# Gate rows and second modulation columns of an adaptive-layernorm block: from TensorE matmuls to VectorE partial products and GpSimd sums over partitions

## Chip, cores, metric

One core of a Trainium2 chip. The metric is the device time of one execution in microseconds (us). Every run here is listed in the state "fast" and with a granted TensorE clock of 1.0 (0.999 in one execution of the kernel before). The profile is one execution taken by the hardware profiler; its span is 1.7 to 1.9 us shorter than the device time.

Ratios are the mean time of one kernel's fast runs over the mean of the other's fast runs of the same rounds, so they are not quite the ratios of the medians quoted beside them. Kernels of one batch ran on the same chip and share the runs of the kernel before.

## The reference

```python
mod = (_silu(c) @ w_mod).reshape(c.shape[0], 6, 1, -1)     # c: 1 x 512, w_mod: 512 x 3072
sa, ca, ga, sb, cb, gb = (mod[:, i].copy() for i in range(6))
h = _layernorm(x, axis=-1) * (1 + ca) + sa                 # x: 1 x 2048 x 512
x = x + ga * _A_ref(h, A_k_cache, A_v_cache, A_wq, A_wo)   # attention, 32 heads, window of 512 keys
h = _layernorm(x, axis=-1) * (1 + cb) + sb
x = x + gb * _B_ref(h, B_w1, B_w2)                         # relu MLP, 512 -> 1792 -> 512
```

(The line with `mod[:, i]` is shortened from six assignments.) The first pair, sa and ca, is needed at once. The gate ga is needed when the first block of 512 rows leaves the output projection, sb and cb before the second layernorm, and gb in the MLP. The change is about these four.

## The kernel before

The attention is a loop of 128 steps, one for each head and block of 512 rows. In a step TensorE makes the scores of head s in two halves, the queries of head s+2, the value product of head s-1, and up to four matmuls from a background queue (`bgq`), mostly the output projection. ScalarE makes the exponentials. VectorE reads the value product out of PSUM, and there is only one place for it (`o_ps`, banks 5 and 6).

```python
def mod_cols_mm(which, bk):          # 32 matmuls of one column: weights stationary, silu(c) moving
    ...
                    fs.append(lambda sl=sl, c2=c2, cc=cc, col=idx * DC + c2, last=last: mm(
                        bank[bk][:, col:col + 1], wm[sl][:, cc, c2 * P:(c2 + 1) * P], sc_bf[:, cc:cc + 1],
                        cc == 0, cc == DC - 1, [R_sc, wm_res(sl, cc)], [bk], last))

def mod_row(j):                      # 4 matmuls of 512 columns: silu(c), repeated 128 times, stationary
    sl, dst, r = (2, gaf, R_ga) if j == 0 else (5, gbf, R_gb)
    for cc in range(DC):
        bgq.append(lambda cc=cc: mm(bank[WBK], sc_rep[:, cc, :], wm[sl][:, cc, :], cc == 0, cc == DC - 1, [R_screp, R_wm[sl]], [WBK], cc == DC - 1))
    evac(lambda: kb.op(DVE, lambda e: e.tensor_copy(dst[:, :], bank[WBK]), reads=[R_b[WBK]], writes=[r]))

def pv_mms(u):                       # value product and its read-out
    ...
    kb.op(DVE, lambda e: e.reciprocal(rinv[:, u, :], o_ps[:, :, P]), ...)
    kb.op(DVE, lambda e: e.tensor_tensor(o_sb[u % NOS][:, :, :], o_ps[:, :, 0:P], ..., op=ALU.mult), ...)
    dma(oT[u % NOT][:, :, :], o_sb[u % NOS]..., transpose=True)

def ln_dmaT():                       # the normalised rows, transposed by DMA
    dma(xnT[...], xn[...], "xnT", reads=R_xn, writes=[R_xnT], transpose=True)

for s in range(NU):
    run_tasks(s, 100)                # VectorE work and loads that are due at step s
    if s == 4:
        mods2()                      # mod_row(0), mod_cols_mm(1, WBK), mod_row(1) into bgq
    ...
    s_mms(s, 0)
    if s + QA < NU:
        q_mms(s + QA)
    s_mms(s, 1)
    if s >= 1:
        pv_mms(s - 1)
    pop_bg(4)
```

`kb.op` records an instruction on an engine's stream with the semaphore waits that its reads and writes need. VectorE takes its stream in order, as the traces show: in the changed kernel a value product ends at 207.85 us, VectorE stands until 209.10 in front of a normalisation, and the reciprocal that reads this product, next in the stream, starts only at 209.75.

## Time and profile before

| | |
|---|---|
| time, median of 4 | 564.17 us (564.06 to 564.25) |
| span of the profile | 562.5 us |
| TensorE / ScalarE / VectorE / GpSimd busy | 553.7 / 350.4 / 242.2 / 38.7 us |

The prediction below shows the page's busy row, the chain that ended last, the groups by shape and the timeline. Two things help in reading them. A reciprocal (`rinv<-psO`) with "idle ... <-PE psO" in brackets started when the value product ended, so the distance between two such rows is the length of a step. A reciprocal without a bracket found VectorE late: the engine came from other work, and TensorE may be waiting for it.

### The profile page before, as it was taken

To read this page: it belongs to the slowest core of one execution; us is meant where nothing else is said; L and a number is where in the kernel's file an instruction comes from. 1 tells how busy PE (TensorE), PEld (TensorE's weight loads), DVE (VectorE), ACT (ScalarE), POOL (GpSimd) and SP (SyncE) were. 2 spreads that over 40 slices of the span, in tenths; PEclk is the share of its full clock that TensorE was granted. 3 is DMA by queue.
4 is the path that set the end of the run, shared out by engine and by line. 5 is a ranking of instruction groups with operands and counts; after the bars stand their busy time and mean duration, and the time that the engine had idled before them with its cause. 6 is when DMAs were issued, how large, how long until landed. Compare 5 with 4: busy or idle time off the path is not lost.

```text
span 562.5 us, 9700 instructions
## 1 busy us (share of the span) xinstructions
PE 553.7 (98%) x4097; PEld 316.9 (56%) x4172; DVE 242.2 (43%) x533; ACT 350.4 (62%) x453; POOL 38.7 (7%) x42
## 2 busy tenths in 40 slices
PE   8999999999999999999999999999999999999998
PEld 3565555555555555555555555555555654444444
DVE  4444465533334655333346553333354448321134
ACT  5986666666666666666666666666666644432500
POOL 1000000003300000033000000330000000000000
PEclk9999999999999999999999999999999999999999
DMA  9778776421331247332523522121123220210001
GB/s 268 204 165 167 143 160 132 113 38 38 39 76 37 39 93 133 57 94 46 144 56 57 102 50 39 39 40 40 39 39 72 44 31 0 41 36 24 22 28 48
DMA packets 113310, 42.70 MB, mean 76 GB/s; under 512 B 93928, under 2 KB 112104, under 8 KB 113256
## 3 DMA queue, kind: packets, MB, share of 16 engines
q1 hardware_dynamic: 112024, 40.82, 35.2%
q10 hardware_dynamic: 1232, 1.15, 0.6%
q8 instruction: 35, 0.57, 0.5%
q14 instruction: 19, 0.16, 0.1%
HBM read 18.35 MB, written 2.10 MB: 36 GB/s over the span
## 4 chain that ended last, share of the span: by engine, by line
PE 97%; issue 1%; DMA 1%; DVE 1%
PE psS L1363 28%; PE psO L1363 26%; PE psQ L1363 23%; PE psW L1363 20%; DMA x<-in_A_x_dram 1%; DVE st L1373 0%; PE psS L1366 0%; DVE mv L1374 0%; DVE rstd L1574 0%; DVE PT L1673 0%; DVE PT L1675 0%; DVE tmp L1427 0%; DVE sc_bf L1428 0%; DVE tmp L1426 0%
## 5 line engine op out<-in xcount | busy, mean ns | idle before, releaser
L1482 ACT ACTIVATE PT<-psS 128x1024 bf16<-128x1024 f32 x256 | 262.6, 1028 | 129.5 <-PE psS L1363 129.4
L1363 PE MATMUL psS<-qT,kT 128*128 128x512 bf16 x509 | 151.1, 379 | 0.2
L1363 PEld LDWEIGHTS psO<-v,PT 128*128 128x128 bf16 x2048 | 126.6, 98 | 30.2
L1363 PE MATMUL psO<-v,PT 128*128 128x129 bf16 x2048 | 137.0, 220 | 0.0
L1363 PE MATMUL psQ<-hT,wq 128*128 128x512 bf16 x507 | 130.3, 379 | 0.1
L1492 DVE RECIPROCAL rinv<-psO 128x4 f32<-128x4 f32 x128 | 23.4, 183 | 233.1 <-PE psO L1363 233.1
L1363 PE MATMUL psW<-wo,oT 128*128 128x512 bf16 x451 | 117.9, 379 | 3.2
L1493 DVE TENSOR_TENSOR o<-psO,rinv 128x512 bf16<-128x512 f32 x128 | 88.5, 692 | 4.4
L1363 PEld LDWEIGHTS psQ<-hT,wq 128*128 128x128 bf16 x508 | 49.6, 98 | 60.7 <-issue 0.5
L1363 PEld LDWEIGHTS psS<-qT,kT 128*128 128x128 bf16 x512 | 49.6, 98 | 59.3 <-ACT PT L1482 0.7
L1474 ACT ACTIVATE qT<-psQ 128x512 bf16<-128x512 f32 x127 | 75.2, 592 | 0.5 <-PE psQ L1363 0.5
L1662 ACT ACTIVATE wq<-psS 128x512 bf16<-128x512 f32 x56 | 33.4, 597 | 49.6 <-PE psS L1363 49.6
L1363 PEld LDWEIGHTS psW<-wo,oT 128*128 128x128 bf16 x512 | 45.0, 98 | 32.9 <-DVE acc L1515 1.2
L1515 DVE TENSOR_TENSOR acc<-psW,acc 128x512 f32<-128x512 f32 x48 | 33.2, 691 | 6.7 <-PE psW L1363 6.7
L1363 PE MATMUL psO<-wmw,wq 128*128 128x512 bf16 (+1 forms) x164 | 32.7, 352 | 0.3
L1518 POOL TENSOR_TENSOR acc<-acc,gaf 128x512 f32<-128x512 f32 x12 | 15.3, 1272 | 168.7 <-DVE acc L1515 168.7
L1379 POOL TENSOR_TENSOR rstd<-rstd,cst 128x4 f32<-128x4 f32 x7 | 7.1, 1012 | 265.3 <-DVE rstd L1378 265.3
L1363 PE MATMUL psS<-h2T,wmw 128*128 128x512 bf16 x110 | 25.2, 379 | 0.1
L1673 DVE TENSOR_TENSOR PT<-psO,gbf 128x512 f32<-128x512 f32 (+1 forms) x12 | 7.5, 624 | 40.4 <-PE psO L1363 40.4
L1363 PEld LDWEIGHTS psO<-wmw,wq 128*128 128x128 bf16 x168 | 15.4, 98 | 16.5
L1363 PE MATMUL psS<-hT,wmw 128*128 128x512 bf16 x110 | 24.4, 379 | 0.1
L1373 DVE BATCH_NORM_STATS2 st<-x 128x6 f32<-128x512 bf16 x31 | 21.0, 678 | 4.8 <-DMA x<-in_A_x_dram 4.8
(73 smaller groups left out, 170.4 us busy)
## 6 DMA issues: line engine op xcount, KB each, us to landing
wo<-in_A_wo_dram SPq DMA_DIRECT2D x4, 1024.0 KB, 5.7
wq<-in_A_wq_dram SPq DMA_DIRECT2D x7, 512.0 KB, 5.7
wmw<-in_B_w_dram SPq DMA_DIRECT2D x14, 256.0 KB, 3.3
wmw<-in_w_mod_dram SPq DMA_DIRECT2D x5, 512.0 KB, 4.7
oT<-o SPq DMA_TRANSPOSE x128, 2.4
out_dram<-PT SPq DMA_DIRECT2D x15, 128.0 KB, 1.8
x<-in_A_x_dram SPq DMA_DIRECT2D x3, 512.0 KB, 4.1
v<-in_A_v_cache_dram SPq DMA_DIRECT2D x8, 128.0 KB, 4.8
```

Of the source, the lines that this page charges most:

```text
L1363: kb.op(PE, lambda e: e.matmul(out_ap, lhsT, rhs, start=start, stop=stop), reads=reads, group_writes=[R_b[k] for k in bk], signal=signal)
L1373: kb.op(DVE, lambda e: e.bn_stats(st[:, t, :], x_sb[:, t, :]), reads=[R_x[t]], writes=[R_st[t]])
L1379: kb.op(POOL, lambda e: e.tensor_tensor(rstd[:, sl], rstd[:, sl], cst[:, 0:1].to_broadcast([P, hi - lo]), op=ALU.pow), reads=R_rstd[sl] + ...
L1474: kb.op(ACT, lambda e: e.activation(qT[u % NQT][:, :], bank[bk], ACTF.Copy), reads=[R_b[bk]], writes=[R_qT[u % NQT]])
L1482: kb.op(ACT, lambda e: e.activation(PT[u % NPT][:, pr * 2:pr * 2 + 2, :], s_ps[pr][:, :, :], ACTF.Exp, scale=scale), reads=[R_b[pr * 2], R ...
L1492: kb.op(DVE, lambda e: e.reciprocal(rinv[:, u, :], o_ps[:, :, P]), reads=[R_b[5], R_b[6]], writes=[R_rinv])
L1493: kb.op(DVE, lambda e: e.tensor_tensor(o_sb[u % NOS][:, :, :], o_ps[:, :, 0:P], rinv[:, u, :].unsqueeze(2).to_broadcast([P, TPB, P]), op=A ...
L1515: kb.op(DVE, lambda e: e.tensor_tensor(acc[:, tl, :], bank[WBK], acc[:, tl, :], op=ALU.add), reads=[R_b[WBK], R_acc[tl]], writes=[R_acc[tl]])
L1518: kb.op(eng, lambda e: e.tensor_tensor(acc[:, tl, :], acc[:, tl, :], gaf[:, :], op=ALU.mult), reads=[R_acc[tl], R_ga], writes=[R_acc[tl]])
L1662: kb.op(ACT, lambda e: e.activation(h1T[b % 2][:, fc, :], bank[bk], ACTF.Relu), reads=[R_b[bk]], writes=[R_h1[b % 2][fc]], pre=all_events( ...
L1673: kb.op(DVE, lambda e: e.tensor_tensor(yt[i][:, c0:c1], bank[bk][:, c0:c1], gbf[:, c0:c1], op=ALU.mult), reads=[R_b[bk], R_gb], writes=[R_ ...
```

## The change

The intent: take 8 wide and 32 narrow matmuls off TensorE, the engine that is 98% busy. Each of the four slices of `w_mod` is multiplied by silu(c) along the partitions and added over its four chunks on VectorE (a "block", one tensor_scalar and three scalar_tensor_tensor). GpSimd sums over the partitions. For sb and cb VectorE picks the diagonals of the result, which turns rows into columns.

```diff
+    def mod_part(sl):
+        dst, r = pr[sl - 2], R_pr[sl - 2]
+        kb.op(DVE, lambda e: e.tensor_scalar(dst, wm[sl][:, 0, :], sc_f[:, 0:1], None, op0=ALU.mult), ...)
+        for cc in range(1, DC):
+            kb.op(DVE, lambda e, cc=cc: e.scalar_tensor_tensor(dst, wm[sl][:, cc, :], sc_f[:, cc:cc + 1], dst, op0=ALU.mult, op1=ALU.add), ...)
+
+    def mod_sum(sl):
+        src, rs = pr[sl - 2], R_pr[sl - 2]
+        kb.op(POOL, lambda e: e.partition_all_reduce(src, src, P, bass_isa.ReduceOp.add), reads=[rs], writes=[rs])
+
+    def mod_col(sl):
+        ...   # multiply by the identity, reduce along the free axis into modc
-    def mods2():
-        mod_row(0)
-        fs = mod_cols_mm(1, WBK)
-        bgq.append(lambda: [f() for f in fs] and None)
-        evac(lambda: mod_cols_evac(1, WBK))
-        mod_row(1)
+    for i, sl in enumerate((2, 3, 4, 5)):
+        add(4 + 2 * i, lambda sl=sl: mod_part(sl))
+    for sl, s in ((2, 12), (3, 24), (4, 36), (5, 58)):
+        add(s, lambda sl=sl: mod_sum(sl))
+    for sl in (3, 4):
+        add(48, lambda sl=sl: mod_col(sl))
```

(Cut: reads and writes, the body of `mod_col`, the new buffers and their resources, and the removal of `mod_row` and of the repeated silu.)

More of the change, by code (lines that the diff above doesn't have):

```diff
@@ L5 @@
 import concourse.bass as bass
+from concourse import bass_isa
 from concourse import mybir
@@ L1258, in build_fast @@
     sc_bf = T("sc_bf", [P, DC])
-    sc_rep = T("sc_rep", [P, DC, P])
+    sc_f = T("sc_f", [P, DC], F32)
     tmp = T("tmp", [P, DC], F32)
@@ L1263, in build_fast @@
     gbf = T("gbf", [P, D], F32)
+    prv = h2T[1][:, :, :].rearrange("p c q -> p (c q)").bitcast(F32)
+    pr = [gaf[:, :], prv[:, 0:D], prv[:, D:2 * D], gbf[:, :]]
     st = T("st", [P, NT, 6], F32)
@@ L1308, in build_fast @@
     R_b = RL("bank", 8)
-    R_ident, R_ones, R_c, R_sc, R_screp, R_tmp, R_cst = (Res(n) for n in ("ident", "ones", "c", "sc", "screp", "tmp", "cst"))
+    R_ident, R_ones, R_c, R_sc, R_scf, R_tmp, R_cst = (Res(n) for n in ("ident", "ones", "c", "sc", "scf", "tmp", "cst"))
     R_moda, R_modb, R_ga, R_gb = Res("moda"), Res("modb"), Res("ga"), Res("gb")
+    R_pr = [R_ga] + RL("pr", 2) + [R_gb]
     R_st, R_mv, R_rstd = RL("st", NT), RL("mv", NT), RL("rstd", NT)
@@ L1444, in mod_cols_evac @@
         kb.op(DVE, lambda e: e.tensor_scalar(modc[:, mo + DC:mo + 2 * DC], bank[bk][:, DC:2 * DC], 1.0, None, op0=ALU.add), reads=[R_b[bk]], writes=[r])
-    def mod_row(j):
-        sl, dst, r = (2, gaf, R_ga) if j == 0 else (5, gbf, R_gb)
-        for cc in range(DC):
-            bgq.append(lambda cc=cc: mm(bank[WBK], sc_rep[:, cc, :], wm[sl][:, cc, :], cc == 0, cc == DC - 1, [R_screp, R_wm[sl]], [WBK], cc == DC - 1))
-        evac(lambda: kb.op(DVE, lambda e: e.tensor_copy(dst[:, :], bank[WBK]), reads=[R_b[WBK]], writes=[r]))
+    def mod_part(sl):
+        dst, r = pr[sl - 2], R_pr[sl - 2]
+        kb.op(DVE, lambda e: e.tensor_scalar(dst, wm[sl][:, 0, :], sc_f[:, 0:1], None, op0=ALU.mult), reads=[R_wm[sl], R_scf], writes=[r])
+        for cc in range(1, DC):
+            kb.op(DVE, lambda e, cc=cc: e.scalar_tensor_tensor(dst, wm[sl][:, cc, :], sc_f[:, cc:cc + 1], dst, op0=ALU.mult, op1=ALU.add),
+                  reads=[R_wm[sl], R_scf, r], writes=[r])
+    def mod_sum(sl):
+        src, rs = pr[sl - 2], R_pr[sl - 2]
+        kb.op(POOL, lambda e: e.partition_all_reduce(src, src, P, bass_isa.ReduceOp.add), reads=[rs], writes=[rs])
+    def mod_col(sl):
+        src, rs = pr[sl - 2], R_pr[sl - 2]
+        o = 2 * DC + (sl - 3) * DC
+        v = src.rearrange("p (c j) -> p c j", c=DC)
+        kb.op(DVE, lambda e: e.tensor_tensor(v, v, ident[:, :].unsqueeze(1).to_broadcast([P, DC, P]), op=ALU.mult), reads=[rs, R_ident], writes=[rs])
+        kb.op(DVE, lambda e: e.tensor_reduce(modc[:, o:o + DC], v, axis=AX.X, op=ALU.add), reads=[rs], writes=[R_modb])
+        if sl == 4:
+            kb.op(DVE, lambda e: e.tensor_scalar(modc[:, o:o + DC], modc[:, o:o + DC], 1.0, None, op0=ALU.add), reads=[R_modb], writes=[R_modb])
     bgq = deque()
@@ L1608, in build_fast @@
     q_mms(1, 5)
-    kb.op(DVE, lambda e: e.tensor_copy(sc_rep[:, :, :], sc_bf[:, :].unsqueeze(2).to_broadcast([P, DC, P])), reads=[R_sc], writes=[R_screp])
+    kb.op(DVE, lambda e: e.tensor_copy(sc_f[:, :], sc_bf[:, :]), reads=[R_sc], writes=[R_scf])
     for g in range(2, G):
@@ L1628, in build_fast @@
         add(s, lambda i=i: load_mlp(i))
-    def mods2():
-        mod_row(0)
-        fs = mod_cols_mm(1, WBK)
-        bgq.append(lambda: [f() for f in fs] and None)
-        evac(lambda: mod_cols_evac(1, WBK))
-        mod_row(1)
+    for i, sl in enumerate((2, 3, 4, 5)):
[4 more added lines that the diff above has]
+        add(48, lambda sl=sl: mod_col(sl))
     for s in range(NU):
         run_tasks(s, 100)
-        if s == 4:
-            mods2()
         if wo_ready and wo_ready[0][0] <= s:
```

## The prediction

Passages are cut, here and in some of the expectations below, each cut marked, because they rested on rules and figures of the hardware that no trace or run shows. The sum of the terms that stand is 564.2 - 2.5 + 3.5 = 565.2 us. Cut are the terms for a slower opening instruction of a block, for a sum on GpSimd that holds up VectorE, and for a much longer sum (rivals b and c). With them the prediction had its middle at 567.0 us and its upper end at 577, and gave "slower by 2%" 18%. Cut is also a deduction of 12 us for two library switches, which left the third sum 17 of its 32 us.

> **What bounds the kernel now.** I read the page first: busy shares, then the chain that ended last.
>
> ```profile
> span 562.5 us, 9700 instructions
> PE 553.7 (98%) x4097; PEld 316.9 (56%) x4172; DVE 242.2 (43%) x533; ACT 350.4 (62%) x453; POOL 38.7 (7%) x42
> ...
> PE 97%; issue 1%; DMA 1%; DVE 1%
> ```
>
> TensorE is busy nearly all the time and carries 97% of the chain, at a granted clock of 1.00 in every stretch. So each microsecond of matmuls removed comes off the time, unless its place is taken by a wait. VectorE (43%) and GpSimd (7%) look free. But that is an average, and VectorE has a deadline in each attention step: the one value accumulator in PSUM must be read out before the next value product may start. The groups by shape give the durations that I use below (busy us, mean ns of one):
>
> ```profile
> L1482 ACT ACTIVATE PT<-psS 128x1024 bf16<-128x1024 f32 x256 | 262.6, 1028 | 129.5 <-PE psS L1363 129.4
> ...
> L1515 DVE TENSOR_TENSOR acc<-psW,acc 128x512 f32<-128x512 f32 x48 | 33.2, 691 | 6.7 <-PE psW L1363 6.7
> ...
> L1518 POOL TENSOR_TENSOR acc<-acc,gaf 128x512 f32<-128x512 f32 x12 | 15.3, 1272 | 168.7 <-DVE acc L1515 168.7
> ...
> L1384 DVE TENSOR_SCALAR xn<-x,mv,rstd 128x512 bf16<-128x512 bf16 x31 | 11.2, 407 | 5.6 <-DMA xnT<-xn 4.5 <-POOL rstd L1379 1.1
> ...
> L1363 PE MATMUL psW<-wmw,sc_rep 128*128 128x512 bf16 x8 | 2.1, 379 | 0.0
> ...
> L1363 PE MATMUL psW<-sc_bf,wmw 128*128 128x1 bf16 x32 | 0.9, 163 | 0.0
> ```
>
> The last two groups are what the change removes. The timeline of 14 to 44 us shows the stretch where they stand (start, duration, engine, line, what; in brackets the idle time before):
>
> ```profile
> 23.40 0.18 DVE L1492 RECIPROCAL rinv<-psO 128x4 f32<-128x4 f32 x1 [0.41 <-PE psO L1363]
> ...
> 23.62 0.69 DVE L1493 TENSOR_TENSOR o<-psO,rinv 128x512 bf16<-128x512 f32 x1
> ...
> 24.23 1.40 DVE L1616 TENSOR_REDUCE vmax<-v 128x1 f32<-128x512 bf16 x2
> ...
> 26.04 0.18 DVE L1492 RECIPROCAL rinv<-psO 128x4 f32<-128x4 f32 x1 [0.41 <-PE psO L1363]
> ...
> 29.53 0.18 DVE L1492 RECIPROCAL rinv<-psO 128x4 f32<-128x4 f32 x1 [1.94 <-PE psO L1363]
> ...
> 32.97 0.18 DVE L1492 RECIPROCAL rinv<-psO 128x4 f32<-128x4 f32 x1 [2.26 <-PE psO L1363]
> ...
> 36.46 0.18 DVE L1492 RECIPROCAL rinv<-psO 128x4 f32<-128x4 f32 x1 [1.94 <-PE psO L1363]
> ...
> 39.09 0.18 DVE L1492 RECIPROCAL rinv<-psO 128x4 f32<-128x4 f32 x1 [0.41 <-PE psO L1363]
> ```
>
> Each reciprocal marks the end of one value product. Its period is 2.63 us in a bare step (36.46 to 39.09, 23.40 to 26.04) and 3.49, 3.44 and 3.49 us in the three steps that carry the modulation matmuls. With its two maxima in the step, VectorE sits idle only 0.41 us of a bare step. That number matters most here.
>
> [...]
>
> **The change part by part.**
>
> Removed from TensorE: 8 matmuls of 512 columns and 32 of one column. Read from the periods: (3.49 - 2.63) + (3.44 - 2.63) + (3.49 - 2.63) = 0.86 + 0.81 + 0.86 = 2.53 us, all on the path. The ScalarE floor of a bare step is 2 x 1.028 + 0.592 = 2.65 us (the exponentials above, and the copies of q at 592 ns), so these three steps fall to 2.65 rather than 2.63; I neglect that. Gain: 2.5 us. VectorE also loses two copies and a small pair, and the replicated silu; none of them was on the path.
>
> Added to VectorE: in each of steps 4, 6, 8 and 10, one tensor_scalar and three scalar_tensor_tensor over 512 columns. With 0.41 us (as the normalisation) and 3 x 0.69 (as the accumulation), plus some 0.03 us between dependent ones, one block is 0.41 + 2.07 + 0.12 = 2.6 us. In program order it stands before the step's own read-out of the value product. VectorE executes in order, so:
> - Step 4: the two maxima end at 24.23 + 1.40 = 25.63; the block ends at 28.25; the read-out (0.18 + 0.69 + gaps = 0.90) ends at 29.15. The product ended near 25.84 (0.2 before the reciprocal), and the next one, with 2.63 - 0.91 = 1.72 us of scores and query matmuls between (0.91 is what the chain, listed in time, has for 16 value matmuls), would start near 27.55. It waits for 29.15: a stall of 1.6 us.
> - Step 8: again two maxima and a block: 1.6 us.
> - Step 6: no maxima, so the block starts 1.40 us earlier, but step 5 ran late: about 0.3 us.
> - Step 10: the output projection has begun (period 3.5 us), so VectorE has 0.86 us more: no stall.
> Sum: +3.5 us. Net with the gain: +1.0 us, 565.2, if nothing else happens.
>
> Added later: the two diagonals at step 48, two products (0.69) and two reductions (0.68) and a small one, about 3.0 us. They hit a 3.49 us step: read-out, accumulation, these and the next read-out make 0.9 + 0.7 + 3.0 + 0.9 = 5.5 us against 2 x 3.49 - 0.90 = 6.08 until the next product. No stall.
>
> Added to GpSimd: four sums over partitions, and, by the instruction order of the built kernel, eight more library switches, one before each sum and one before the ordinary work behind it. GpSimd waits only for data, so a sum starts when its turn comes, not at its numbered step: the first at about 28.3 us when block one ends (its library loaded long before), the second after the power for block 1 (82.9), the third after the first gated row tile (133.3), the fourth after the second power (202.4). What ordinary work must follow in time:
>
> ```profile
> 81.90 1.01 POOL L1379 TENSOR_TENSOR rstd<-rstd,cst 128x4 f32<-128x4 f32 x1 [73.35 <-DVE rstd L1378]
> ```
>
> The first sum has 81.9 - 28.3 = 53 us with a switch behind it. The third delays the three gated tiles behind it, which the accumulator copy at 165 needs: 165 - 133 = 32 us[...]. Inside those lengths none of this reaches TensorE.
>
> [...]
>
> **The rivals.**
> (a) Pure gain, 561.7: VectorE's 57% of idle time would swallow the blocks. Against it: the 0.41 us above, and in-order execution. It would hold if the chip's vector blocks ran faster than 2.2 us.
> [...]
> [...]
>
> **How range and chances follow.**[...] Low end 563: half the stalls absent.[...] Faster by 2% would need 552.9, though all removed work is 2.5 us: 1%.[...] Within 2%: 81%.
>
> **What would show it.** The TensorE row without the two removed groups, and 2.5 us less busy. Reciprocals after the first and third block about 1.6 us late, with waits of TensorE for the read-out of the value product in those steps, where before had none. Block instructions at 0.41 and 0.69 us[...].[...] I am wrong if TensorE shows no waits near steps 4 to 8, or if waits stand near the powers, the gated tiles or step 48.

## More of the kernel before

A third stretch came to matter only after the result, the layernorms near 200 us. Rows of the timeline, start, duration, engine or queue, what; SPq is the queue that issues the transposes:

```profile
201.30 1.95 SPq L1297 DMA_TRANSPOSE xnT<-xn  x1
...
205.72 0.74 DVE L1384 TENSOR_SCALAR xn<-x,mv,rstd 128x512 bf16<-128x512 bf16 x2 [2.24 <-DMA xnT<-xn]
```

Two layernorms follow each other through one buffer there. The second may only write `xn` when the transpose of the first has landed, so VectorE stands for 2.24 us, in order, in front of the next read-out of a value product. This just fits: TensorE does not stop.

## The result

The changed kernel is correct and takes 567.86 us (567.6 to 568.25, 4 runs) against 564.17: ratio 1.0066, 95% interval 1.0051 to 1.0081. It is 0.7% slower.

The page of the changed kernel, for the lines of the page that the prediction shows:

```profile
span 566.3 us, 9730 instructions
...
PE 555.3 (98%) x4132; PEld 314.5 (56%) x4132; DVE 254.3 (45%) x550; ACT 350.5 (62%) x453; POOL 51.9 (9%) x46
...
PE 90%; DMA 4%; DVE 4%; issue 1%; DVEq 0%
```

TensorE's matmul count says nothing of the removed matmuls, because some matmul records are missing in a trace: it shows 4132 here and 4097 before, although 40 were removed. The weight loads (PEld) show them: 4172 before, 4132 now. The chain says what became of the time: TensorE's share fell from 97% to 90%, and DMA and VectorE now have 4% each. What ends last is no longer TensorE's work alone.

The groups by shape, for the new work:

```profile
L1459 POOL PARTITION_ALL_REDUCE h2T<-h2T x2 | 6.5, 3248 | 12.7 <-issue 12.7
...
L1454 DVE SCALAR_TENSOR_TENSOR gaf<-wmw,sc_f,gaf 128x512 f32<-128x512 bf16 x3 | 2.3, 751 | 0.1
...
L1452 DVE TENSOR_SCALAR h2T<-wmw,sc_f 128x512 f32<-128x512 bf16 x2 | 1.3, 664 | 0.0
L1452 DVE TENSOR_SCALAR gbf<-wmw,sc_f 128x512 f32<-128x512 bf16 x1 | 0.5, 478 | 0.0
```

A sum takes 3.25 us. The block's opening instruction takes 0.48 us, yet two of them average 0.66: one was held up. The timeline of VectorE from 20 to 60 us shows which, and what the blocks do to the read-outs:

```profile
24.41 1.39 DVE L1634 TENSOR_REDUCE vmax<-v 128x1 f32<-128x512 bf16 x2
25.72 0.48 DVE L1452 TENSOR_SCALAR gaf<-wmw,sc_f 128x512 f32<-128x512 bf16 x1
26.24 2.33 DVE L1454 SCALAR_TENSOR_TENSOR gaf<-wmw,sc_f,gaf 128x512 f32<-128x512 bf16 x3
28.48 0.18 DVE L1510 RECIPROCAL rinv<-psO 128x4 f32<-128x4 f32 x1
...
30.55 0.18 DVE L1510 RECIPROCAL rinv<-psO 128x4 f32<-128x4 f32 x1 [1.17 <-PE psO L1367]
...
31.38 0.85 DVE L1452 TENSOR_SCALAR h2T<-wmw,sc_f 128x512 f32<-128x512 bf16 x1
...
36.58 0.18 DVE L1510 RECIPROCAL rinv<-psO 128x4 f32<-128x4 f32 x1 [1.18 <-PE psO L1367]
...
43.55 0.18 DVE L1510 RECIPROCAL rinv<-psO 128x4 f32<-128x4 f32 x1 [1.17 <-PE psO L1367]
```

The reciprocal at 28.48 has no bracket: VectorE came late from the block, 2.26 us later than a bare step would have it. Between the bracketed ones, which stand at the end of a value product, two bare steps should take 2 x 2.63 = 5.26 us. They take 30.55 - 23.59 = 6.96 (23.59 is the bracketed row before the first one shown), then 6.03, then 6.97. So the three stalls are 1.70, 0.77 and 1.71 us, 4.18 together; from 43.55 on the steps are as long as before. TensorE's own timeline shows who is waited for, and the one of GpSimd shows what held the second block:

```profile
29.43 1.08 PE L1367 MATMUL psO<-v,PT 128*128 128x129 bf16 x16 [1.53 <-DVE o L1511]
...
35.47 1.08 PE L1367 MATMUL psO<-v,PT 128*128 128x129 bf16 x16 [0.59 <-DVE o L1511]
...
42.43 1.08 PE L1367 MATMUL psO<-v,PT 128*128 128x129 bf16 x16 [1.53 <-DVE o L1511]
```

```profile
28.70 3.25 POOL L1459 PARTITION_ALL_REDUCE gaf<-gaf  x1 [19.97 <-DVE rinv L1510]
83.73 1.06 POOL L1383 TENSOR_TENSOR rstd<-rstd,cst 128x4 f32<-128x4 f32 x1 [51.78 <-DVE rstd L1382]
91.72 3.25 POOL L1459 PARTITION_ALL_REDUCE h2T<-h2T  x1 [6.92 <-issue]
...
210.22 3.38 POOL L1459 PARTITION_ALL_REDUCE gbf<-gbf  x1 [5.96 <-issue]
```

The first sum runs from 28.70 to 31.95, and the block's opening instruction of 31.38 falls into it. The 6.92 and 5.96 us of "issue" in front of the other sums shown are the library switches: at the head of each (85.01 and 204.47 us) the trace records two MODIFY_POOL_CONFIG on GpSimd, and it has 18 of these where the trace of before has 2.

The kernel is not 4.18 - 2.53 = 1.65 us slower, though, but 3.7. I compared the times of all 128 reciprocals with those of before. The lag is 1.8 us from step 10 up to 206 us, 3.4 us behind that, and 4.1 us behind 325 us. In both later stretches VectorE waits for a transpose. Timeline of the first, in the changed kernel:

```profile
203.12 1.99 SPq L1300 DMA_TRANSPOSE xnT<-xn  x1
...
209.10 0.73 DVE L1388 TENSOR_SCALAR xn<-x,mv,rstd 128x512 bf16<-128x512 bf16 x2 [3.80 <-DMA xnT<-xn]
...
211.17 1.76 DVE L1388 TENSOR_SCALAR xn<-x,mv,rstd 128x512 bf16<-128x512 bf16 x2
```

From the issue to the start of the waiting work were 4.42 us before (201.30 to 205.72); now they are 5.98. And the second pair of normalisations takes 1.76 us instead of the 0.73 of the first pair; the last sum, 210.22 to 213.60, lies over it. The change touches neither the transpose nor its neighbours. The view of the DMA queues for just this stretch, in the changed kernel, has one line more than that of the same stretch of before:

```profile
q1 hardware_dynamic: 3128, 0.78, 87.9%
q8 instruction: 1, 0.02, 0.9%
```

One packet of 16 KB on an instruction queue. In the whole trace such a packet stands on this queue every 16 us or so. The times of these fetches (from the trace's DMA packets), against the issue of the transposes that VectorE waits for (us from the span's start):

```
kernel    issue    waiting work starts   fetches around it
before    201.30   205.72                199.4   216.0
before    313.20   317.62                311.3   327.4
changed   203.12   209.10                207.1
changed   316.63   322.61                320.6
```

A matmul is two rows in the profile, weight load and multiply, so the 40 removed matmuls are 80 rows. Between two fetches from 60 to 470 us the trace of before records 107 to 138 weight loads, 126 on average, so some 250 rows. 80 rows are about a third of that, which is 5 us of the 16 (an estimate from these counts). The changed kernel's fetches at 207.1 and 320.6 stand 7.7 and 9.3 us behind those of before at 199.4 and 311.3; less the lag of 1.8 and 3.4 us that is 5.9 both times. That the packets carry TensorE's instructions is an inference, which the experiments test. This gave the theory for the experiments.

**Theory F:** removing the matmuls moved TensorE's instruction fetches onto the two transposes, which then land 1.5 us late; VectorE, already waiting there, has no room for it. **Rival V:** the late transposes come from the work that the change added on VectorE and GpSimd. **Rival N** on the early stalls: the blocks cost their time wherever they stand, as a second bound.

### The profile page after: what moved, and what is told of

Same layout as the page of the kernel before. It is cut to its first block, busy times and chain, and to the rows that moved or that the text cites. A ratio compares the mean times of both kernels' runs of the same rounds, so it can differ in the third digit from the quotient of the medians.

```text
span 566.3 us, 9730 instructions
## 1 busy us (share of the span) xinstructions
PE 555.3 (98%) x4132; PEld 314.5 (56%) x4132; DVE 254.3 (45%) x550; ACT 350.5 (62%) x453; POOL 51.9 (9%) x46
## 4 chain that ended last, share of the span: by engine, by line
PE 90%; DMA 4%; DVE 4%; issue 1%; DVEq 0%
PE psS L1367 26%; PE psO L1367 25%; PE psQ L1367 21%; PE psW L1367 19%; DMA xnT<-xn 4%; DVE o L1511 1%; DMA x<-in_A_x_dram 1%; DVE xn L1388 0%; DVE vmax L1634 0%; DVE gaf L1454 0%; DVE st L1377 0%; DVE h2T L1454 0%; DVE rinv L1510 0%; DVE acc L1533 0%; PE psS L1370 0%
## 5 line engine op out<-in xcount | busy, mean ns | idle before, releaser
L1367 PE MATMUL psW<-wo,oT 128*128 128x512 bf16 x512 | 130.6, 379 | 0.0
```

Of the source, the lines that this page charges most:

```text
L1367: kb.op(PE, lambda e: e.matmul(out_ap, lhsT, rhs, start=start, stop=stop), reads=reads, group_writes=[R_b[k] for k in bk], signal=signal)
```

## Experiments

"Empty instructions" are no-operations on TensorE's stream. They change where the fetches fall and nothing else, except for the time that they take themselves. In the table "lag" is how much later than in the kernel before the reciprocals stand in the profiled run (negative: earlier): behind step 10, behind the layernorms near 210 us, and behind those near 325 us. "hit" says whether a fetch fell 3.9 to 4.1 us behind the issue of the transpose.

| run | time us | ratio | lag, step 10 | lag, 2nd | lag, 3rd | hit |
|---|---|---|---|---|---|---|
| changed | 567.86 | 1.0066 | +1.8 | +3.4 | +4.1 | yes |
| matmuls removed only | 563.20 | 0.9983 | -2.4 | -1.8 | -1.2 | yes |
| the same + 96 empty | 563.85 | 0.9992 | -0.6 | -0.6 | -0.6 | no |
| changed + 96 empty | 567.75 | 1.0061 | +3.7 | +3.7 | +3.7 | no |
| before + 170 empty in batches | 566.98 | 1.0046 | +1.5 | +2.2 | +2.9 | yes |
| before + 170 empty, spread | 565.24 | 1.0022 | -0.1 | +0.6 | +1.2 | yes |
| changed without sums | 566.55 | 1.0047 | +1.2 | +1.8 | +2.5 | yes |
| last sum early | 566.99 | 1.0052 | +1.6 | +2.2 | +2.8 | yes |
| blocks moved | 563.98 | 0.9994 | -2.4 | -0.6 | +0.1 | yes |
| blocks moved, sums in a row | 563.13 | 0.9985 | -2.5 | -1.9 | -1.2 | yes |
| the same + 96 empty, spread | 561.61 | 0.9954 | -2.6 | -2.6 | -2.6 | no |

The half-widths of the intervals of the ratios are 0.0012 to 0.0016 for all of them. The medians of the kernel before were 564.0, 564.08 and 564.03 in the three batches.

### Matmuls removed, nothing in their place

```diff
 def mods2():
-    mod_row(0)
-    ... (all modulation matmuls and their read-outs)
+    kb.op(POOL, lambda e: e.memset(gaf[:, :], 1.0), writes=[R_ga])
+    kb.op(POOL, lambda e: e.memset(gbf[:, :], 1.0), writes=[R_gb])
+    kb.op(POOL, lambda e: e.memset(modc[:, 2 * DC:4 * DC], 1.0), writes=[R_modb])
```

Wrong: the gates are 1.

> The 8 wide and 32 narrow modulation matmuls are gone and nothing stands in their place (gates and second modulation are set to 1, so the result is wrong on purpose); VectorE and GpSimd have none of the new work. Theory F (fetch): TensorE's instructions come in 16 KB fetches, one each 16 us; with 80 fewer instructions they fall 6 us later in the program, onto the transposes of the normalised rows near 203 and 317 us, which then land in 6.0 instead of 4.3 us. F expects the three steps 2.5 us shorter, but some 2.3 us back at the two transposes: 563.5 to 564.5 us. Rival V (the late transposes come from the change's work on VectorE and GpSimd): the transposes land in 4.3 us and the time is 561.7.

Measured: 563.20 us, ratio 0.9983. The three steps are 0.86, 0.80 and 0.86 us shorter, 2.52 in all; the prediction's reading of 2.53 us from the periods is exact. Half of it is gone again at the two transposes (0.62 and 0.57 us), which land late although neither VectorE nor GpSimd has any of the new work (the three memsets run before 10 us):

```profile
204.84 0.74 DVE L1384 TENSOR_SCALAR xn<-x,mv,rstd 128x512 bf16<-128x512 bf16 x2 [3.78 <-DMA xnT<-xn]
```

That speaks against V. F's range was missed by 0.3 us all the same: it expected some 2.3 us back, and 1.2 came back, because the steps behind make up part of the 1.5 us.

### The same with 96 empty instructions

```diff
     s_mms(s, 1)
+    if s < 4:
+        for _ in range(24):
+            PE.ops.append((lambda e: e.nop(hint="phase", nofuse=True), [], []))
```

> As the run with the matmuls removed, with 96 empty instructions spread over TensorE's first four steps, so that the later fetches fall about 6 us earlier, where they were in the kernel before. F: both transposes land in 4.3 us, 561.7 us (if the empty instructions themselves cost nothing). V: the same as without the empty instructions.

Measured: 563.85 us, no gain, and so the expected time was missed. The mechanism held all the same: the waits at the transposes are 2.23 us again, and the lag does not change between step 10 and the end. But the batches of empty instructions were not free: the third reciprocal is 1.92 us late, on average 20 ns for each (1.42 us of it behind the first two batches). That is more than the 1.2 us they saved.

### The changed kernel with the same 96

> The changed kernel with the same 96 empty instructions. F: the transposes land in 4.3 us; 1.5 to 2.3 us less than the changed kernel, 565.6 to 566.4 us (what the last sum[...] costs near 211 us stays). V: 567.9 us, transposes at 6.0 us.

Measured: 567.75 us, outside F's range and next to the 567.9 that V named, so the time alone decides nothing. It is again too high by the cost of the empty instructions (2.09 - 0.18 = 1.9 us in the lag of the third reciprocal). The trace decides: both transposes land in 4.3 us. The lag is +3.7 behind step 10 and stays so to the end: both later stretches cost nothing now, where they cost 1.6 and 0.7 us in the changed kernel. So the long second pair of normalisations is gone too, which I had not expected. When the transpose is on time, that pair ends before the last sum begins, if only just (212.24 against 212.40). The long pair near 211 us (1.76 us in the changed kernel, 0.72 here) was a consequence of the late transpose.

### The kernel before, its fetches moved onto the transposes

The same edit on the kernel before, 17 empty instructions in each of the first ten steps; nothing else changed.

> The kernel before, all its work untouched, with 170 empty instructions on TensorE in the first ten steps, so that its fetches near 216 and 327 us come about 10 us earlier, onto the transposes at 201 and 313 us. F: these land in about 6 us, VectorE waits 3.8 instead of 2.2 us for them, 566 to 567 us. V: nothing of that, 564.2 us.

Measured: 566.98 us. The fetches stand at 206.9 and 319.4, the transposes land late, and the untouched kernel shows the wait of the changed one:

```profile
208.88 0.74 DVE L1388 TENSOR_SCALAR xn<-x,mv,rstd 128x512 bf16<-128x512 bf16 x2 [3.90 <-DMA xnT<-xn]
```

Of the loss, 1.5 us are lag before the first transpose (0.4 of it stand before the first empty instruction, the rest is theirs) and 1.4 the transposes, so the time alone would not prove much. The cleaner version spreads them:

```diff
 def mm(...):
     kb.op(PE, ...)
+    if shift[0] > 0 and (bk[0] < 4 or bk[0] == QBK):   # set to 170 when the loop begins
+        shift[0] -= 1
+        PE.ops.append((lambda e: e.nop(hint="phase", nofuse=True), [], []))
```

> The kernel before with 170 empty instructions again, but one behind each wide matmul of scores and queries, so that they cost nothing. What is left is the fetches moved onto the two transposes, with no other work changed: F expects the reciprocals level with the kernel before up to 200 us, then 0.6 us behind, then 1.2 us: 565.3 us.

Measured: 565.24 us, ratio 1.0022 (1.0009 to 1.0036). One behind each wide matmul, they cost nothing that shows (lag -0.1 up to 201 us), and the two stretches cost 0.7 and 0.6 us. So the place of the fetches alone makes 1.2 us of this kernel's time. F stands: over all kernels of the table and the kernel before, a fetch hit 16 of these transposes, and VectorE waits 3.7 to 3.9 us for each; it missed 8, and VectorE waits 2.2 to 2.3 us.

The packets in the traces show how. In each of the 16 hit transposes, 7 to 12 packets of 256 bytes, which take 18 ns in the median, took over 1 us, the longest 1.4 to 1.55 us. They began 4.2 to 4.4 us behind the issue, while the packet of 16 KB was moving (0.88 to 0.93 us), and the last 34 or 35 packets started only after 4.7 us. In the 8 missed ones no such packet took more than 0.15 us.

### The sums taken away

```diff
 def mod_sum(sl):
-    kb.op(POOL, lambda e: e.partition_all_reduce(src, src, P, bass_isa.ReduceOp.add), reads=[rs], writes=[rs])
+    pass
```

Its output is wrong, which doesn't matter for the time.

> The changed kernel with its four VectorE blocks but without the four sums on GpSimd (so no library switches; the gates and columns are wrong on purpose). If the first sum[...] is what made the opening instruction of the second block 0.85 instead of 0.48 us: it takes 0.48, the second stall shrinks from 0.77 to about 0.4 us, the first and third stay at 1.7. The transposes still land late; without the last sum[...]: 567.9 - 0.4 - 0.9 = 566.6 us. Rival (the 0.85 us has another cause, such as the late load of the third weight slice): it stays.

Measured: 566.55 us. The opening instruction of the second block takes its 0.48 us:

```profile
31.14 0.48 DVE L1452 TENSOR_SCALAR h2T<-wmw,sc_f 128x512 f32<-128x512 bf16 x1
```

The second stall is 35.97 - 30.32 - 5.26 = 0.39 us instead of 0.77. So it is the first sum that held this instruction up; that cost 0.4 us, of which 0.37 are seen directly in the instruction.

### The last sum directly behind the third

```diff
-    for sl, s in ((2, 12), (3, 24), (4, 36), (5, 58)):
+    for sl, s in ((2, 12), (3, 24), (4, 36), (5, 36)):
```

> The changed kernel with the last sum directly behind the third (two library switches fewer), nothing else moved. If the 1.0 us that the second pair of normalisations took longer near 211 us was[...] the last sum: that pair takes 0.73 us again, the late transposes stay at 6.0 us, and the gain of the second stretch over the first shows: about 0.9 us less than the changed kernel, 567.0 us. Rival (the pair was long because of the library switch or the transposes): pair still 1.7 us, 567.9.

Measured: 566.99 us; the second pair of normalisations takes 0.73 us at 210.90, and the step from 206 to 217 us costs 0.6 us instead of 1.6. The transposes still land late. What the last sum did to the pair was worth 0.9 to 1.0 us.

### The blocks moved into longer steps

```diff
-        add(4 + 2 * i, lambda sl=sl: mod_part(sl))
+        add((10, 13, 14, 18)[i], lambda sl=sl: mod_part(sl))
```

> The changed kernel with its four VectorE blocks in steps 10, 13, 14 and 18, where the output projection makes a step 0.86 us longer and no maxima stand, instead of 4, 6, 8 and 10; the sums keep their places in GpSimd's queue. If the stalls of the first steps (4.2 us by the reciprocals) come from the blocks standing before the read-out in short steps: they vanish, the times of the reciprocals run 2.5 us ahead of the kernel before by step 20, and the two late transposes (fetch)[...] remain: 563.5 to 564.2 us. Rival: the blocks cost TensorE their time wherever they stand (VectorE as a second bound): 567 to 568.

Measured: 563.98 us, 3.9 us less than the changed kernel by this one line. The reciprocals run 2.37 us ahead of the kernel before until 206 us; one or two behind a block are up to 0.9 us later, and the next step makes it up. So all four blocks are hidden, with the same VectorE work (and the first sum no longer lies on block two, 0.4 of the 3.9 us). N falls. What is left at the end is the fetch, and the last sum, which still lies on the second pair (1.88 us at 207.03).

### Blocks moved and the sums in one row; and with the fetches shifted

```diff
-        add(4 + 2 * i, lambda sl=sl: mod_part(sl))
-    for sl, s in ((2, 12), (3, 24), (4, 36), (5, 58)):
+        add((10, 11, 13, 14)[i], lambda sl=sl: mod_part(sl))
+    for sl, s in ((5, 15), (2, 15), (3, 15), (4, 15)):
```

The sum of the last block is first in GpSimd's queue, so that no sum lies on a block.

> Blocks in steps 10, 11, 13 and 14 and all four sums in one row behind the last block (two library switches instead of eight). Expected: no stalls from the blocks,[...] only the fetch's 1.2 us on the two transposes: as the run with the matmuls removed, 562.9 to 563.3 us. If the sums in a row reach past the power at 82 us, or block VectorE: 565 or more.

Measured: 563.13 us, what the removal alone gives (563.20). The four sums stand from 57.77 to 70.69 us, and the power at 79.44 is not late. Only two library switches remain.

> The same with 96 empty instructions, one behind each of TensorE's first 96 wide matmuls of scores and queries, so that the fetches miss the transposes. In batches of 24 these cost 1.9 us (20 ns each); spread out, each lies behind a matmul of 216 ns and should cost nothing: 561.7 us, transposes at 4.3 us. If each still costs 20 ns: 563.6.

Measured: 561.61 us (561.43 to 562.25), ratio 0.9954 (0.9941 to 0.9968): correct, and 0.5% faster than the kernel before. The page:

```profile
span 559.9 us, 9739 instructions
...
PE 97%; issue 1%; DMA 1%; DVE 1%
```

The chain is TensorE's again, and the 2.5 us are the whole of the removed matmuls.

## Why the prediction was right, and where not

The measured 567.86 lies in the range (563 to 577), 0.9 us from the forecast of 567.0 and 2.7 us from the 565.2 of the terms that stand. The forecast was nearly right for partly wrong terms:

| term | predicted us | measured us |
|---|---|---|
| matmuls removed | -2.5 | -2.52 (removal alone) |
| stall of step 4 | +1.6 | +1.70 |
| stall of step 6, without the sum | +0.3 | +0.39 |
| stall of step 8 | +1.6 | +1.71 |
| stall of step 10, diagonals at step 48 | 0 | 0 (0.16 late for one step, then made up) |
| block two held up under the first sum | cut | +0.38 |
| normalisations held up under the last sum | not named | +1.0 |
| late transposes by instruction fetch | not named | +0.6 and +0.6 |

- **Removal and stalls** held, step by step. The argument that carried it was the 0.41 us of VectorE idle time in a bare step with two maxima; VectorE's 57% of idle time, rival (a), was no guide. The blocks were 0.25 us longer than estimated (2.84 instead of 2.6): 0.75 us instead of 0.69 for a scalar_tensor_tensor, 0.48 instead of 0.41 for the opening.
- **Block two under the first sum**: the first sum began at 28.70, where the forecast had 28.3, and takes 3.25 us. The opening instruction of block two begins under it at 31.38 and takes 0.85 us instead of 0.48, at a cost of 0.4 us. The trace of before has one overlap of this kind: two normalisations at 8.11 and 8.43 run under a power of GpSimd (7.79 to 8.56) and take their usual 0.41 us. As the legend of the profile calls spans on GpSimd rough, it settles little.
- **The later sums**: the forecast placed the fourth sum after the second power, and so did the trace. It did not ask which work of VectorE the fourth meets. Without the late transpose these normalisations are early enough, by 0.16 us.
- **What the forecast missed** is that fewer instructions move the later fetches of the program, the two at the transposes by 5.9 us. It took VectorE and TensorE behind step 48 for unchanged, and 2.3 us of the lag arose there. That they came near the some 2 us by which the cut terms had raised the forecast is chance.
- **Sums and signs that do not hold.** With the cut terms the sum came to 568 to 569; the middle of 567 was not worked out from it. A bare step of 2.63 us cannot have a ScalarE floor of 2.65, and the three steps fell to 2.63. For rival (a) a block would have to be as short as 1.0 us by the prediction's own working (2.6 less the stall of 1.6), not 2.2. Of the signs, "TensorE 2.5 us less busy" did not show (555.3 us after 553.7, with records missing).

The ledger: -2.5 + 4.2 + 1.2 + 1.0 + 0.2 (the first reciprocal is already late by 0.18 us) = 4.1 us, which is the lag of the last reciprocal. The spans differ by 3.8. The last 0.3 us need no cause in the change: from the last reciprocal to the end the trace of before takes 105.55 us, the changed kernel 105.23, and before with spread empty instructions 105.25.

That moving the fetch moves the delay is shown, and so are the transpose's packets that stand still meanwhile. The trace does not tell which DMA engine a packet used; why the packets stand still is not shown.

## What to carry to other kernels

Work that moves from a full engine to an idle one costs nothing only if the idle time lies where the work is put. Look for the shortest deadline that the receiving engine serves in that very step, not at its share of the span; one line that named other steps was worth 3.9 us here. Before trusting a difference below 1% as an effect of an edit, check whether something at the other end of the program has moved: here the number of instructions decided whether an instruction fetch met a critical transfer, which was 1.2 us either way, and 2.3 with the conflict that it caused.

## What these runs measured

- The sum over partitions at 128 x 512 fp32 took 3.25 to 3.38 us. In front of the sums stand 5.8 to 6.9 us of idle time for the library switch (up to 8.1 in the variants), and where the return to ordinary work waited for nothing else, it cost as much again (6.83 us in front of a gated tile, 6.70 with the last sum early).
- VectorE work under a sum took longer: 0.85 instead of 0.48 us for the opening instruction, a pair of normalisations 1.76 instead of 0.73. But the held work did not wait for the recorded end of the sum: both normalisations of that pair ended by 212.93, the first in 1.44 us and the second in its usual 0.40, and the sum is recorded until 213.60. As recorded spans on GpSimd are rough, whether the pair is held for the whole instruction stays open, and what holds it is not shown.
- A transpose hit by an instruction fetch let VectorE start 1.5 us later (5.98 us from issue instead of 4.42).
- What no-operations on TensorE cost depended on the place: 1.9 us for 96 in four batches of 24, some 1.1 us for 170 in ten batches of 17, nothing that shows when one stood behind each 512-column matmul.
- A scalar_tensor_tensor with a bf16 and an fp32 input took 751 ns over 512 columns.
